# A decode-attention kernel: V trails K by two units instead of three, and older heads' projections move ahead of the last weighted sums

## The chip, the cores and the metric

The kernel runs on one core of one Trainium2 chip. The metric is the device time of one execution in microseconds, the median over several executions. The profile gives a second number, the span from the first to the last instruction.

Names used below: PE is the TensorE matmul engine, DVE is VectorE, ACT is ScalarE, POOL is GpSimd, and SP is SyncE, which issues the loads here. All times inside an execution are counted from the start of its span.

## The reference, cut to what matters

There are two independent attention blocks, A and B. Each has 2 batch entries, 32 heads, head size 192, model width 640, one new token and a cache of 8192 positions, in bf16. For each block:

```python
q = (x @ wq)                                   # [2, 1, 32*192], per head
scores = einsum("bhqd,bhkd->bhqk", q, k_cache) * 192 ** -0.5
p = softmax(scores)
o = einsum("bhqk,bhkd->bhqd", p, v_cache)      # the weighted sum
out = o.reshape(2, 1, 32*192) @ wo             # the projection
```

A pair of (head, batch entry) is a *unit*; there are 128. A unit has 3.1 MB of K and 3.1 MB of V, and each byte is used once.

## The kernel before: the parts that matter

SP issues all loads in one fixed order. Two K buffers and two V buffers hold one unit each. A load waits until its buffer is free: K until DVE has multiplied the old K by q, V until PE has finished the old weighted sum. This is the order ("LAG" is the trail of V behind K):

```python
LAG = cfg.get("LAG", 3)
LATE = LAG - 1
...
for u in range(NU):
    korder.append(("k", u))
    lag = min(1 + u // 8, LAG)        # 1, then 2, then 3
    while u - lag >= nv:
        korder.append(("v", nv)); nv += 1
for u in range(nv, NU):
    korder.append(("v", u))           # what is left: the last V, one after another
```

The work of every engine is sorted by *slot*, then by an order number within the slot. The weighted sum of unit `u` stands in PE's slot `u + LATE`. The traces show PE's work in this order, and where one instruction waited, those behind it waited too (e7 below: a projection waited 1.19 us for ACT, and PE stood idle for as long).

```python
put(pe_tab, u + LATE, 0, pe_pv(u, ...), ...)           # weighted sum: 32 matmuls
...
# near the end V is loaded in pieces, each with its own semaphore (T = 64 rows per partition)
for i, cuts in enumerate(((32, 64), (32, 64), (16, 32, 48, 64), (16, 32, 48, 56, 64))):
    PCS[NU - 4 + i] = (n0, cuts)                       # units 124, 125, 126, 127
def v_tile(u):                                         # V of the last two units goes to K buffers
    return kb[u % NK] if NU >= 8 and u >= NU - 2 else vb[u % NV]
```

Every two heads (four units) a finished group goes through five steps: ACT copies the sums out of PSUM (`f1`), PE transposes them with matmuls of one column (`f3`, 6 in the code and 12 in the trace, where each fp32 matmul shows as two passes), ACT scales by 1/sum (`f4`), and PE multiplies by `wo` (`f5`, 6 matmuls). DVE's `f2` is the reciprocal. Near the end these stand as follows. Group 30 ("older heads") covers units 120 to 123, and group 31 ("last pair") covers 124 to 127:

```python
at = u1 + 2 + LATE                                     # u1: last unit of the group
if pp == LASTP:                                        # group 31, split in three
    put(pe_tab, at - 1, 1, pe_f3h(0), ...)             # first head: after the last sum
    put(pe_tab, at - 1, 2, pe_f3h(1, (0,)), ...)       # second head, batch 0: after the last sum
    put(pe_tab, at, 1, pe_f3h(1, (1,)), ...)           # second head, batch 1
    put(act_tab, at - 1, 4, act_f4(pp, (0,)), ...)
    put(act_tab, at + 2, 3, act_f4(pp, (1,)), ...)
else:
    put(pe_tab, at, 1, pe_f3, ...)                     # group 30: between the sums of 125 and 126
    put(act_tab, at + 2, 3, act_f4(pp), ...)
put(pe_tab, at + 1, 2, pe_f5(pp), ...)                 # group 30: between the sums of 126 and 127
```

The streams of PE, DVE and ACT are emitted with hardware loops over the regular middle part. In these loops an engine waits on a semaphore against a value in a register.

Of the kernel before, what the change touches and what calls it, by code (L numbers as in the profile page):

```python
# [102 lines left out]
def build_kernel(nc, blocks, out, cfg=None):  # L103
    cfg = dict(cfg or {})
# [9 lines left out]
    NU = G * B  # L114
    scale = float(Dh) ** -0.5

    NA_MAIN = min(cfg.get("NA", 16), T - 2)
    LAG = cfg.get("LAG", 3)
    LATE = LAG - 1
    NPB = 4  # L120
    NK = cfg.get("NK", 2)
# [26 lines left out]
    with ExitStack() as es:  # L148
# [41 lines left out]
        S_pool = _Stream("pool", sem("s_pool"), reg)  # L190
        ksem = [sem(f"ksem{i}") for i in range(NK)]
        vsem = [sem(f"vsem{i}") for i in range(NV)]
        NTAIL = 13
        vtail = [sem(f"vtail{i}") for i in range(NTAIL)]
        k0sem = sem("k0sem")
        wq0sem = sem("wq0sem")
# [5 lines left out]
        def key(name, *idx):  # L202
            for i in idx:
                if i < 0:
                    return None
            return (name,) + tuple(idx)
# [6 lines left out]
            reg[("wo", w)] = (wosem, 16 * (w + 1))  # L213
        PCS = {}
        if NU >= 8:
            for i, cuts in enumerate(((32, 64), (32, 64), (16, 32, 48, 64), (16, 32, 48, 56, 64))):
                n0 = sum(len(c) for _, c in PCS.values()) if PCS else 0
                PCS[NU - 4 + i] = (n0, cuts)

        def pieces(u):  # L220
            if u not in PCS:
# [54 lines left out]
            return dma(kb[u % NK][:, ks:T, :], src[:, ks:T, :], KSPLIT[u])  # L276

        def v_tile(u):
            return kb[u % NK] if NU >= 8 and u >= NU - 2 else vb[u % NV]

        def sp_v(u, t0=0, t1=None, sm=None):
            blk, h, b, g = unit(u)
# [54 lines left out]
        def act_f1(g):  # L337
            hs = g % 2

            def fn(eng):  # L340
                eng.activation(o_sb[0:1, :, hs, :], ops[hs][0:1, :, 0:Dh], ACTF.Identity)  # L341
                return eng.activation(o_sb[32:33, :, hs, :], ops[hs][32:33, :, Dh:2 * Dh], ACTF.Identity)  # L342
            return fn

        def act_f1b(g, b):
            hs = g % 2

            def fn(eng):
                eng.activation(o_sb[0:1, b, hs, :], ops[hs][0:1, b, 0:Dh], ACTF.Identity)
                return eng.activation(o_sb[32:33, b, hs, :], ops[hs][32:33, b, Dh:2 * Dh], ACTF.Identity)  # L350
            return fn
# [47 lines left out]
        def pe_pv(u, j0, j1):  # L399
            b = u % B  # L400
            vv = v_tile(u)[:].rearrange("p (j a) d -> p j (a d)", a=2)

            def fn(eng):
                for j in range(j0, j1):
                    ins = eng.matmul(ops[(u // B) % 2][0:33, b, 0:QW], pb[u % NPB][:, j, :], vv[:, j, :],  # L405
                                     start=(j == 0), stop=(j == T // 2 - 1))
                return ins
            fn.same = (j0, j1)
            return fn
# [49 lines left out]
        def put(tab, slot, order, fn, waits, sig):  # L459
            tab[slot].append((order, len(tab[slot]), fn, waits, sig))  # L460

        for u in range(NU):
            g = u // B
            put(dve_tab, u + 1, 0, dve_d3(u), [("acc", u), ("r", u), key("ar", u - 2)], ("d3", u))
            put(dve_tab, u, 2, dve_d1a(u), [("k", u), ("a0", qg_of(u)), key("acc", u - 2)], ("d1a", u))
            put(dve_tab, u, 3, dve_d1b(u), [("k", u), ("kb", u) if u in KSPLIT else None, ("a0", qg_of(u)),
                                            key("r", u - 1)], ("d1b", u))
            put(dve_tab, u, 4, dve_lvl(u, 96), [("d1b", u)], ("l1", u))
            put(dve_tab, u, 5, dve_lvl(u, 48), [("l1", u)], ("l2", u))
            put(dve_tab, u, 6, dve_lvl(u, 24), [("l2", u)], ("l3", u))  # L470
            put(dve_tab, u, 7, dve_r(u), [("l3", u), key("d3", u - 2), key("exp", u - 2)], ("r", u))
            put(pool_tab, u + 1, 0, pool_ar(u), [("d3", u), key("nb", u - 2)], ("ar", u))
            put(pool_tab, u + 1, 1, pool_ls(u), [("exp", u), key("f2", g - 2)], ("ls", u))
            put(act_tab, u + 1, 0, act_nb(u), [("ar", u), key("exp", u - 2)], ("nb", u))
            put(act_tab, u + 1, 1, act_exp(u), [("nb", u), ("acc", u), ("r", u), key("pv", u - NPB)], ("exp", u))
            for t in range(na_of(u)):
                w = [("d1a", u), key("d3", u - 2), key("exp", u - 2)] if t == 0 else []
                put(act_tab, u, 10 + t, act_acc(u, t), w, ("acc", u) if t == na_of(u) - 1 else None)
            pc = pieces(u)
            w0 = [("exp", u), key("f1", g - 2), ("init",)]  # L480
            if pc is None:
                put(pe_tab, u + LATE, 0, pe_pv(u, 0, T // 2), w0 + [("v", u)], ("pv", u))
            else:
                for i, (t0, t1, sm) in enumerate(pc):
                    put(pe_tab, u + LATE, 0, pe_pv(u, t0 // 2, t1 // 2), (w0 if i == 0 else []) + [("vp", u, i)],
                        ("pv", u) if i == len(pc) - 1 else None)

        LASTP = G // 2 - 1 if G >= 4 else -99
        for g in range(G):
            u1 = 2 * g + 1  # L490
            pp = g // 2
            at = u1 + 2 + LATE
            w1 = [key("f3", pp - 1), ("init",)]
            if pp == LASTP and g % 2 == 0:
                put(act_tab, at + 1, 2, act_f1(g), [("pv", u1)] + w1, ("f1", g))
            elif pp == LASTP:
                put(act_tab, at - 1, 3, act_f1b(g, 0), [("pv", u1 - 1)] + w1, ("f1a", g))
                put(act_tab, at, 2, act_f1b(g, 1), [("pv", u1), ("f1a", g)], ("f1", g))
            else:
                put(act_tab, at, 2, act_f1(g), [("pv", u1)] + w1, ("f1", g))  # L500
            put(dve_tab, u1 + 2, 8, dve_f2(g), [("ls", u1), key("f4", pp - 2)], ("f2", g))
        for pp in range(G // 2):
            g1 = 2 * pp + 1
            u1 = 2 * g1 + 1
            at = u1 + 2 + LATE
            w4 = [("f2", g1 - 1), ("f2", g1), ("init",), ("wo", (2 * pp) // HG)]
            if pp == LASTP:
                put(pe_tab, at - 1, 1, pe_f3h(0), [("f1", g1 - 1), key("f4", pp - 1), ("init",)], ("f3a", pp))
                put(pe_tab, at - 1, 2, pe_f3h(1, (0,)), [("f1a", g1)], ("f3b", pp))
                put(pe_tab, at, 1, pe_f3h(1, (1,)), [("f1", g1), ("f3b", pp)], ("f3", pp))  # L510
                put(act_tab, at - 1, 4, act_f4(pp, (0,)), [("f3b", pp)] + w4, ("f4a", pp))
                put(act_tab, at + 2, 3, act_f4(pp, (1,)), [("f3", pp), ("f4a", pp)] + w4, ("f4", pp))
            else:
                put(pe_tab, at, 1, pe_f3, [("f1", g1 - 1), ("f1", g1), key("f4", pp - 1), ("init",)], ("f3", pp))
                put(act_tab, at + 2, 3, act_f4(pp), [("f3", pp), key("f5", pp - 1)] + w4, ("f4", pp))
            w = [("f4", pp), key("f5", pp - 1)]
            put(pe_tab, at + 1, 2, pe_f5(pp), w, ("f5", pp))
            if g1 % Hn == Hn - 1:
                blk = g1 // Hn
                to = at + 3 if blk == NBLK - 1 else NU - 4  # L520
                put(act_tab, to, 95, act_out(blk), [("f5", pp)], ("oev", blk))
                put(act_tab, to, 96, act_out_dma(blk, 0), [("oev", blk)], None)
                put(act_tab, to, 97, act_out_dma(blk, 1), [("oev", blk)], None)
# [7 lines left out]

        def add_v(u):
            pc = pieces(u)
            w = [("d1b", u)] if NU >= 8 and u >= NU - 2 else [key("pv", u - NV)]
            if pc is None:
                S_sp.add(sp_v(u), waits=w)
            else:
                for (t0, t1, sm) in pc:
                    S_sp.add(sp_v(u, t0, t1, sm), waits=w)
# [15 lines left out]
        for kind, u in korder:  # L555
            if kind == "k":
                if u in KSPLIT:
                    S_sp.add(sp_k(u, 0), waits=[key("d1b", u - NK)])
                    S_sp.add(sp_k(u, 1))
                else:  # L560
                    S_sp.add(sp_k(u), waits=[key("d1b", u - NK)])
                if u == 0:
                    if WQSPLIT:
                        S_sp.add(sp_wq(0, 1))
                    for blk in range(1, NBLK):
                        for b in range(B):
                            S_sp.add(sp_x(blk, b))
                w = u // UG
                if u % UG == (5 if UG >= 8 else 1):
                    S_sp.add(sp_wo(w), waits=[key("f5", (w - 1) * HG // 2)])  # L570
                if u % UG == (3 if UG >= 8 else 0) and w + 1 < NWG:
                    S_sp.add(sp_wq(w + 1), waits=[key("pq", w * HG)])
            else:
                add_v(u)
# [90 lines left out]
```

## Time and profile before

| | before |
|---|---|
| time, median of 3 executions | 1961.84 us (1961.54 to 1963.42) |
| the execution that was profiled | time 1963.61, span 1961.8 |
| bytes moved | 837 MB |
| DMA rate in the middle | 428 to 435 GB/s |
| busy: DVE, PE, ACT | 84%, 57%, 46% of the span |
| last piece of V(127) complete | 1951.70 |
| last weighted sum ends | 1955.19 |

The page of the kernel before: its first line, and the rows of 40 time slices for the DMA (tenths of busy share, then GB/s).

```profile
span 1961.8 us, 18371 instructions
...
DMA  9999999999999999999999999999999999999997
GB/s 371 429 430 431 432 430 433 431 430 433 431 433 433 429 432 433 431 433 431 432 430 431 432 430 433 431 432 428 435 432 431 432 430 433 431 432 431 432 432 299
```

The DMA's busy share is 9 tenths or more in 39 of the 40 slices, and its rate is flat: 428 to 435 GB/s in 38 of them. Only two slices are low: the first (371), where the loads start up (246 GB/s in the first 10 us), and the last (299). PE waited 774 us in all for landings of V, and DVE 236 us for landings of K. So the DMA is what the body waits for, and the end is worth looking at. This is the chain of waits of the kernel before from 1937 us on (start, duration, what; xN is the number of instructions):

```profile
1937.03 2.78 PE ops L405 x16
1939.81 2.18 PE oTps L414 x12
1941.99 6.98 PE ops L405 x32
1948.97 0.91 PE outps L441 x6
1949.88 5.31 PE ops L405 x32
1955.19 1.36 PE oTps L425 x18
...
1957.42 0.70 PE oTps L425 x6
...
1958.46 0.99 PE outps L441 x6
```

`ops L405` are weighted sums, first the second half of unit 125, then 126, then 127. `oTps L414` and `outps L441` between them are the older heads' transposes and projection. PE works without a pause although the data is there: PE, not the DMA, ends last. Two numbers describe the end:

- from the last landing to the end of the last sum: 1955.19 - 1951.70 = 3.5 us;
- from there to the end of the span: 1961.8 - 1955.19 = 6.6 us.

The landing times come from the trace's semaphore records. Each of these last loads left 16 of them, and the kernel waits for a count of 16. They are read here as one for each of the 16 DMA engines that the page counts. For the last piece the first engine was done at 1946.80, the fifteenth at 1949.39 and the sixteenth at 1951.70. The sixteenth is what the work waits for. So a load counts as landed at its sixteenth record.

### The profile page before, as it was taken

What the parts mean: (1) busy time and instruction counts of PE and PEld (TensorE: products, weight loads), DVE (VectorE), ACT (ScalarE), POOL (GpSimd) and SP (SyncE); (2) the same over time, 40 slices, a digit from 0 to 9 for tenths busy, and PEclk for the clock granted to TensorE, in tenths of its full rate; (3) what the DMA queues carried; (4) which work ended last, traced back from release to release, by engine and by line L of the source; (5) the groups of instructions that cost most, each with busy time, mean ns of one, the idle gap of its engine ahead of it and who ended that gap; (6) DMA issues with size and microseconds to landing.
All of it is one profiled execution on the core that took longest, in us unless ns stands there. A gap on an engine that the chain in (4) does not pass through costs nothing.

```text
span 1961.8 us, 18371 instructions
## 1 busy us (share of the span) xinstructions
PE 1115.6 (57%) x5004; PEld 590.1 (30%) x5004; DVE 1656.0 (84%) x962; ACT 903.0 (46%) x4743; POOL 172.8 (9%) x270
## 2 busy tenths in 40 slices
PE   2445546655566555655655556556564665556657
PEld 1222223332333223322333333223332332223324
DVE  7889898888888888898888988888888888888884
ACT  4445444445444444454444444444445444544442
POOL 3013030000001000000000000000000000000000
PEclk9777777777777777777777777777777777777778
DMA  9999999999999999999999999999999999999997
GB/s 371 429 430 431 432 430 433 431 430 433 431 433 433 429 432 433 431 433 431 432 430 431 432 430 433 431 432 428 435 432 431 432 430 433 431 432 431 432 432 299
DMA packets 56476, 837.12 MB, mean 427 GB/s; under 512 B 7416, under 2 KB 18304, under 8 KB 23680
## 3 DMA queue, kind: packets, MB, share of 16 engines
q1 hardware_dynamic: 56432, 836.79, 99.7%
q8 instruction: 12, 0.20, 0.0%
q14 instruction: 16, 0.13, 0.0%
q10 hardware_dynamic: 16, 0.01, 0.0%
HBM read 836.77 MB, written 0.01 MB: 427 GB/s over the span
## 4 chain that ended last, share of the span: by engine, by line
DMA 72%; PE 22%; DVE 5%; issue 1%; SPq 0%; ACT 0%; DVEq 0%
DMA vb<-in_B_v_cache_dram 35%; DMA vb<-in_A_v_cache_dram 29%; PE ops L405 22%; DMA kb<-in_A_k_cache_dram 8%; DVE prodD L309 3%; DVE prodD L316 1%; DVE prodA L305 0%; DVE sc L320 0%; PE oTps L414 0%; PE oTps L425 0%; PE outps L441 0%; SPq L242 0%; SPq L249 0%; DVE mp L312 0%; ACT oTzL L359 0%
## 5 line engine op out<-in xcount | busy, mean ns | idle before, releaser
L405 PE MATMUL ops<-vb,pb 128*33 128x384 bf16 x4032 | 939.9, 408 | 774.1 <-DMA vb<-in_B_v_cache_dram 387.5
L405 PEld LDWEIGHTS ops<-vb,pb 128*33 128x33 bf16 x4032 | 473.4, 120 | 1231.5 <-DMA vb<-in_B_v_cache_dram 405.8
L327 ACT ACTIVATE prodA<-prodA 128x192 bf16<-128x192 bf16 x2048 | 709.0, 350 | 117.0 <-DVE prodA L305 116.8
L309 DVE TENSOR_TENSOR prodD<-kb,qbc 128x9216 bf16<-128x9216 bf16 x128 | 633.7, 4951 | 3.6 <-DMA kb<-in_A_k_cache_dram 3.6
L316 DVE TENSOR_TENSOR prodD<-prodD 128x4608 bf16<-128x4608 bf16 (+2 forms) x384 | 599.0, 1560 | 13.3
L305 DVE TENSOR_TENSOR prodA<-kb,qbc 128x3072 bf16<-128x3072 bf16 x128 | 225.2, 1759 | 238.9 <-DMA kb<-in_B_k_cache_dram 126.9
L327 ACT ACTIVATION_READ_ACCUMULATOR prodA<-prodA 128x1 f32 x2048 | 386.9, 189 | 0.0
L331 ACT ACTIVATE nb<-mg 128x1 f32<-128x1 f32 x128 | 25.9, 203 | 737.0 <-POOL mg L292 737.0
L292 POOL PARTITION_ALL_REDUCE mg<-mp x128 | 56.3, 440 | 1637.5 <-DVE mp L312 1637.5
L320 DVE TENSOR_REDUCE sc<-prodD 128x48 f32<-128x1152 bf16 x128 | 173.2, 1353 | 4.4
L296 POOL PARTITION_ALL_REDUCE lall<-rs x128 | 105.6, 825 | 114.7 <-ACT pb L334 114.7
L387 PE MATMUL qps<-wqs,xbc 128*128 (+1 forms) x320 | 67.9, 347 | 53.4 <-ACT qbc L365 42.4
L414 PEld LDWEIGHTS oTps<-ones,o_sb 33*128 33x128 f32 x372 | 67.1, 258 | 9.8 <-issue 9.8
L414 PE MATMUL oTps<-ones,o_sb 33*128 33x1 f32 x372 | 69.8, 311 | 0.0
L341 ACT ACTIVATE o_sb<-ops 1x384 f32<-1x384 f32 x63 | 29.9, 475 | 86.0 <-PE oTps L414 75.5
L365 ACT ACTIVATE qbc<-qps 128x384 bf16<-128x384 f32 x64 | 31.3, 488 | 77.4 <-PE qps L387 76.7
L334 ACT ACTIVATE pb<-sc,nb 128x64 bf16<-128x64 f32 x128 | 52.2, 408 | 16.6 <-ACT nb L331 8.3
L387 PEld LDWEIGHTS qps<-wqs,xbc 128*128 128x128 bf16 x320 | 27.2, 101 | 88.7 <-ACT qbc L365 44.3
L312 DVE TENSOR_REDUCE mp<-sc 128x1 f32<-128x64 f32 x128 | 28.2, 220 | 13.7 <-issue 4.7
L441 PE MATMUL outps<-wos,oTz 128*4 (+1 forms) x186 | 31.1, 304 | 15.1 <-ACT oTz L359 15.1
L342 ACT ACTIVATE o_sb<-ops 1x384 f32<-1x384 f32 x63 | 30.3, 481 | 0.7
L334 ACT ACTIVATION_READ_ACCUMULATOR pb<-sc,nb 128x1 f32 x128 | 23.8, 186 | 0.0
(27 smaller groups left out, 78.1 us busy)
## 6 DMA issues: line engine op xcount, KB each, us to landing
vb<-in_A_v_cache_dram SPq DMA_DIRECT2D x64, 3072.0 KB, 22.2
kb<-in_B_k_cache_dram SPq DMA_DIRECT2D x64, 3072.0 KB, 23.0
kb<-in_A_k_cache_dram SPq DMA_DIRECT2D x63, 3072.0 KB, 22.5
vb<-in_B_v_cache_dram SPq DMA_DIRECT2D x60, 3072.0 KB, 22.8
wos<-in_A_wo_dram SPq DMA_DIRECT2D x8, 960.0 KB, 26.8
wqs<-in_B_wq_dram SPq DMA_DIRECT2D x8, 960.0 KB, 24.5
wos<-in_B_wo_dram SPq DMA_DIRECT2D x8, 960.0 KB, 26.8
wqs<-in_A_wq_dram SPq DMA_DIRECT2D x7, 960.0 KB, 24.5
```

The costliest lines, as they stand in the source:

```text
L292: return lambda eng: eng.partition_all_reduce(mg[u % 2][:], mp[u % 2][:], 128, bass.bass_isa.ReduceOp.max)
L296: return lambda eng: eng.partition_all_reduce(lall[g % 2][:, b:b + 1], rs[u % 2][:], 128, bass.bass_isa.ReduceOp.add)
L305: return lambda eng: eng.tensor_tensor(prodA[u % 2][:, 0:na, :], kb[u % NK][:, 0:na, :], qb_bc(u, na), ALU.mult)
L309: return lambda eng: eng.tensor_tensor(prodD[:, 0:T - na, :], kb[u % NK][:, na:T, :], qb_bc(u, T - na), ALU.mult)
L316: return lambda eng: eng.tensor_tensor(prodD[:, 0:nd, 0:w], prodD[:, 0:nd, 0:w], prodD[:, 0:nd, w:2 * w], ALU.add)
L320: return lambda eng: eng.tensor_reduce(sc[u % 2][:, na:T], prodD[:, 0:T - na, 0:24], AXL.X, ALU.add)
L327: return lambda eng: eng.activation(prodA[u % 2][:, t, :], prodA[u % 2][:, t, :], ACTF.Identity, accum_out=sc[u % 2][:, t:t + 1])
L334: return lambda eng: eng.activation(pb[u % NPB][:, :, ::32], sc[u % 2][:].rearrange("p (j a) -> p j a", a=2), ACTF.Exp, bias=nb[u % 2][:], ...
L365: return lambda eng: eng.activation(qbc[qg % 4][:], qps[:, 0:QW].rearrange("p (a d) -> p a d", a=2), ACTF.Identity)
L387: ins = eng.matmul(qps[:, 0:QW], xbc[blk][b][:, c, :], wqs[:, slot, c, off].rearrange("p a n -> p (a n)") if slot is not w % 2 else wqs[:, ...
L405: ins = eng.matmul(ops[(u // B) % 2][0:33, b, 0:QW], pb[u % NPB][:, j, :], vv[:, j, :], start=(j == 0), stop=(j == T // 2 - 1))
L414: ins = eng.matmul(oTps[:, 2 * i + b:2 * i + b + 1], o_sb[:, b, :, :].rearrange("p s (r i) -> p i (s r)", i=3)[:, i, :], ones33[:], start= ...
```

## The change

The intent is to have PE follow the arriving V pieces closely at the end and to leave as little as possible behind the last one. The core of the diff:

```diff
-    LAG = cfg.get("LAG", 3)
+    LAG = cfg.get("LAG", 2)
...
-            for i, cuts in enumerate(((32, 64), (32, 64), (16, 32, 48, 64), (16, 32, 48, 56, 64))):
-                PCS[NU - 4 + i] = (n0, cuts)
+            for i, cuts in enumerate(((16, 32, 48, 64), (16, 32, 48, 64), (16, 32, 48, 56, 64))):
+                PCS[NU - 3 + i] = (sum(len(c) for _, c in PCS.values()), cuts)
...      # V(126) goes to a K buffer, V(127) to the V buffer of unit 124
...      # last pair: copies, transposes and first scaling
-                put(act_tab, at + 1, 2, act_f1(g), ...)
+                put(act_tab, u1 + 3, -1, act_f1(g), ...)
-                put(act_tab, at - 1, 3, act_f1b(g, 0), ...)
+                put(act_tab, u1 + 1, 3, act_f1b(g, 0), ...)
-                put(pe_tab, at - 1, 1, pe_f3h(0), ...)
-                put(pe_tab, at - 1, 2, pe_f3h(1, (0,)), ...)
+                put(pe_tab, u1 + LATE, -1, pe_f3h(0), ...)        # before the sum of 127
+                put(pe_tab, u1 + LATE, 0.25, pe_f3h(1, (0,)), ...) # between pieces of 127
-                put(act_tab, at - 1, 4, act_f4(pp, (0,)), ...)
+                put(act_tab, u1 + 1, 4, act_f4(pp, (0,)), ...)
...      # older heads (near = group 30)
-                put(pe_tab, at, 1, pe_f3, ...)
-                put(act_tab, at + 2, 3, act_f4(pp), ...)
-            put(pe_tab, at + 1, 2, pe_f5(pp), ...)
+                put(pe_tab, at - 1 if near else at, -1 if near else 1, pe_f3, ...)    # before the sum of 124
+                put(act_tab, at if near else at + 2, 3, act_f4(pp), ...)
+                put(pe_tab, at if near else at + 1, -1 if near else 2, pe_f5(pp), ...) # before the sum of 125
...
-                if u % UG == (5 if UG >= 8 else 1):     # when the output weights are loaded
+                if u % UG == (4 if UG >= 8 else 1):
```

With a trail of two the last loads are K(127), V(125), V(126), V(127). With three they were K(127), V(124), V(125), V(126), V(127).

More of the change, by code (lines that the diff above doesn't have):

```diff
@@ L192, in build_kernel @@
         vsem = [sem(f"vsem{i}") for i in range(NV)]
-        NTAIL = 13
+        NTAIL = 15
         vtail = [sem(f"vtail{i}") for i in range(NTAIL)]
@@ L215, in build_kernel @@
         if NU >= 8:
-            for i, cuts in enumerate(((32, 64), (32, 64), (16, 32, 48, 64), (16, 32, 48, 56, 64))):
-                n0 = sum(len(c) for _, c in PCS.values()) if PCS else 0
-                PCS[NU - 4 + i] = (n0, cuts)
+            for i, cuts in enumerate(((16, 32, 48, 64), (16, 32, 48, 64), (16, 32, 48, 56, 64))):
+                PCS[NU - 3 + i] = (sum(len(c) for _, c in PCS.values()), cuts)
         def pieces(u):
@@ L278, in v_tile @@
         def v_tile(u):
-            return kb[u % NK] if NU >= 8 and u >= NU - 2 else vb[u % NV]
+            if NU >= 8 and u == NU - 2:
+                return kb[u % NK]
+            if NU >= 8 and u == NU - 1:
+                return vb[(u - 3) % NV]
+            return vb[u % NV]
         def sp_v(u, t0=0, t1=None, sm=None):
@@ L484, in build_kernel @@
                 for i, (t0, t1, sm) in enumerate(pc):
-                    put(pe_tab, u + LATE, 0, pe_pv(u, t0 // 2, t1 // 2), (w0 if i == 0 else []) + [("vp", u, i)],
+                    put(pe_tab, u + LATE, 0.1 * i, pe_pv(u, t0 // 2, t1 // 2), (w0 if i == 0 else []) + [("vp", u, i)],
                         ("pv", u) if i == len(pc) - 1 else None)
@@ L494, in build_kernel @@
             if pp == LASTP and g % 2 == 0:
-                put(act_tab, at + 1, 2, act_f1(g), [("pv", u1)] + w1, ("f1", g))
+                put(act_tab, u1 + 3, -1, act_f1(g), [("pv", u1)] + w1, ("f1", g))
             elif pp == LASTP:
-                put(act_tab, at - 1, 3, act_f1b(g, 0), [("pv", u1 - 1)] + w1, ("f1a", g))
+                put(act_tab, u1 + 1, 3, act_f1b(g, 0), [("pv", u1 - 1)] + w1, ("f1a", g))
                 put(act_tab, at, 2, act_f1b(g, 1), [("pv", u1), ("f1a", g)], ("f1", g))
@@ L506, in build_kernel @@
             w4 = [("f2", g1 - 1), ("f2", g1), ("init",), ("wo", (2 * pp) // HG)]
+            w5 = [("f4", pp), key("f5", pp - 1)]
             if pp == LASTP:
-                put(pe_tab, at - 1, 1, pe_f3h(0), [("f1", g1 - 1), key("f4", pp - 1), ("init",)], ("f3a", pp))
-                put(pe_tab, at - 1, 2, pe_f3h(1, (0,)), [("f1a", g1)], ("f3b", pp))
+                put(pe_tab, u1 + LATE, -1, pe_f3h(0), [("f1", g1 - 1), key("f4", pp - 1), ("init",)], ("f3a", pp))
+                put(pe_tab, u1 + LATE, 0.25, pe_f3h(1, (0,)), [("f1a", g1)], ("f3b", pp))
                 put(pe_tab, at, 1, pe_f3h(1, (1,)), [("f1", g1), ("f3b", pp)], ("f3", pp))
-                put(act_tab, at - 1, 4, act_f4(pp, (0,)), [("f3b", pp)] + w4, ("f4a", pp))
+                put(act_tab, u1 + 1, 4, act_f4(pp, (0,)), [("f3b", pp)] + w4, ("f4a", pp))
                 put(act_tab, at + 2, 3, act_f4(pp, (1,)), [("f3", pp), ("f4a", pp)] + w4, ("f4", pp))
+                put(pe_tab, at + 1, 2, pe_f5(pp), w5, ("f5", pp))
             else:
-                put(pe_tab, at, 1, pe_f3, [("f1", g1 - 1), ("f1", g1), key("f4", pp - 1), ("init",)], ("f3", pp))
-                put(act_tab, at + 2, 3, act_f4(pp), [("f3", pp), key("f5", pp - 1)] + w4, ("f4", pp))
-            w = [("f4", pp), key("f5", pp - 1)]
-            put(pe_tab, at + 1, 2, pe_f5(pp), w, ("f5", pp))
+                near = pp == LASTP - 1
+                put(pe_tab, at - 1 if near else at, -1 if near else 1, pe_f3,
+                    [("f1", g1 - 1), ("f1", g1), key("f4", pp - 1), ("init",)], ("f3", pp))
+                put(act_tab, at if near else at + 2, 3, act_f4(pp), [("f3", pp), key("f5", pp - 1)] + w4, ("f4", pp))
+                put(pe_tab, at if near else at + 1, -1 if near else 2, pe_f5(pp), w5, ("f5", pp))
             if g1 % Hn == Hn - 1:
@@ L533, in add_v @@
             pc = pieces(u)
-            w = [("d1b", u)] if NU >= 8 and u >= NU - 2 else [key("pv", u - NV)]
+            w = [key("pv", u - NV)]
+            if NU >= 8 and u == NU - 2:
+                w = [("d1b", u)]
+            if NU >= 8 and u == NU - 1:
+                w = [("pv", u - 3)]
             if pc is None:
```

## The prediction

> **What bounds the kernel now.** The DMA. The page shows a mean DMA share of 9 tenths or more in 39 of 40 slices and 430 to 433 GB/s in nearly all of them; 837 MB have to be moved. [...] DVE is busy 84% and PE 57%, and both wait for landings. So reordering can shorten only head and tail.
>
> **The body (units 16 to about 123).** A unit moves 6.3 MB in about 14.6 us. Today V(u-3) follows K(u) and the sum of u stands in slot u+2; afterwards V(u-2) follows K(u) and the sum stands in slot u+1. Seen from the transfers, PE does the same work at the same time, and buffers come free as before. The scores of u are ready about 14.3 us after K(u) lands (timeline), V(u) lands about 36 us after K(u). No new wait. Gain 0.
>
> **The head.** The trace shows PE waiting 15.5, 17.0 and 13.6 us for ACT in the first 155 us. The new slots remove most of this, but the windows show DMA share 1.0 from 10 us on, so it is worth about 0.
>
> **The tail.** In the timeline PE works without a break from 1937.03 to 1956.54, with data waiting: sum of unit 125's second half 2.78, older heads' transpose 2.18, unit 126's sum 6.98, older heads' output projection 0.91, unit 127's sum 5.31 (ends at 1955.19), transposes 1.36. The landings in the trace: the last piece of V(127) is complete at 1951.70 (its first engine was done at 1946.80; one engine trails). [...] So 3.5 us of PE work lie behind the last byte, then 6.6 us to the end (1961.8).
>
> After: three V instead of four follow the last K; older heads' transpose (2.18) and projection (0.91) are done before the last sums; two of three parts of the last transpose (estimate 0.9 and 0.45) go ahead of, or between, the last pieces. K(127) lands about 7.3 us later, at about 1929; its softmax is then done at about 1944, before the first piece of V(127) (1946.1). PE then follows the pieces: a piece of 8 matmuls costs 1.3 us at full clock and about 1.9 throttled, pieces come every 1.83 us. The last sum should end about 1.3 us after the last landing (at about 1953), and the chain behind it shrinks from 6.6 to about 5.0 us (copy 0.6, transpose 0.75, scale 0.3, projection 1.0, output copy 0.45, output DMA 1.9). Landings stay: same bytes, as many pieces.
>
> Sum: 1961.8 - 2.2 - 1.6 = **1958 us**, range 1955 to 1961. Chances: faster by over 2%: 0.005; within 2%: 0.99; slower: 0.005.
>
> **What would show it.** Right: last V landing within 1 us of 1951.7 and body slices unchanged; PE's last sum waits for the DMA piece by piece; the chain of waits goes from the last V piece through few matmuls into copy, transpose, projection. Wrong: PE's last sum waits for the last softmax (K(127) late), or PE is still running without a break behind the pieces at a throttled clock, or body slices lose GB/s.
>
> **What would make it wrong.** A lower PE clock in the last 10 us (32 matmuls took 5.3 to 8.2 us), a different trail of the slowest DMA engine, or the last softmax later than 1946.

The sum came to 1958.0 us: from 1961.8 it takes 2.2 us (3.5 to 1.3, behind the last landing) and 1.6 us (6.6 to 5.0, the chain after it).

## The result, and the profile after

The time is 1958.24 us, the median of 4 executions (1957.15 to 1959.41), against 1961.69 (1960.63 to 1963.42, 4 executions) before. The ratio is 0.9982, with a 95% interval of 0.9964 to 0.9999, just clear of 1. The difference of the medians is 3.45 us; the prediction's was 3.8.

The page of the kernel after, its first line and the GB/s of the slices:

```profile
span 1955.3 us, 18519 instructions
...
GB/s 385 430 433 428 433 431 432 433 430 432 431 432 432 431 434 430 432 433 429 432 430 433 431 430 433 431 431 434 429 433 430 432 433 432 431 429 435 432 433 338
```

The middle is unchanged. The first slice is 14 GB/s higher and the last 39. The chain of waits of the kernel after, its end:

```profile
1928.14 18.52 DMA vb<-in_B_v_cache_dram
...
1946.71 1.48 PE ops L408 x8
1948.19 0.61 PE oTps L428 x6
1948.80 1.42 PE ops L408 x8
...
1950.95 0.70 PE oTps L428 x6
...
1951.99 0.99 PE outps L444 x6
```

Now a DMA landing at 1946.67 (the third of V(127)'s five pieces) is on the chain, and behind it stand only 16 matmuls of the last sum and three transposes (6 passes). The last piece landed at 1948.53 and the last sum ended at 1950.22, 1.7 us behind it. From there to the end are 5.1 us.

| profiled executions | before | after | difference |
|---|---|---|---|
| last landing | 1951.70 | 1948.53 | -3.2 |
| last landing to end of the last sum | 3.5 | 1.7 | -1.8 |
| end of the last sum to end of the span | 6.6 | 5.1 | -1.5 |
| span | 1961.8 | 1955.3 | -6.5 |

The profiled pair differs by 6.5 us and the medians by 3.45. So about half of what the pair shows, the earlier last landing, needs an explanation of its own. Adding up the packets of the load queue in the order of their ends shows where most of that half comes from: 15 MB had been moved 1.7 us earlier in the kernel after (40.86 against 42.60), and 1.6 to 2.0 us separate the two at 50, 500 and 834 MB. At 4 MB (14.08 us) there was no gap yet, at 10 MB it was 1.5 us (29.18 against 30.73). The windows view of that stretch, for the kernel before (PE, PE's weight loads, DVE, ACT and POOL busy with their counts; the last three numbers are the clock granted to PE as a share of full speed, the DMA share and GB/s):

```profile
15.00:30.00 15.00, 1.78 (x5) 0.59 (x5) 14.76 (x8) 3.24 (x20) 9.18 (x4) 1.00 0.99 378
```

and for the kernel after:

```profile
15.00:30.00 15.00, 0.00 (x0) 0.00 (x0) 14.76 (x8) 3.06 (x19) 9.13 (x4) 0.50 0.99 423
```

The DMA is busy in both, at 378 and 423 GB/s. The loads issued up to 33 us are the same ones in the same order, at times that differ by 0.04 us or less. Either the change causes this in some other way, or it is chance. The experiments below show which.

### The profile page after: what moved, and what is told of

The parts are those of the page before. It is cut to its first block, busy times and chain, and to the rows that moved or that the text cites. A ratio compares the mean times of both kernels' runs of the same rounds, so it can differ in the third digit from the quotient of the medians.

```text
span 1955.3 us, 18519 instructions
## 1 busy us (share of the span) xinstructions
PE 1110.9 (57%) x5004; PEld 588.5 (30%) x5004; DVE 1656.2 (85%) x962; ACT 903.2 (46%) x4743; POOL 165.8 (8%) x270
## 4 chain that ended last, share of the span: by engine, by line
DMA 74%; PE 23%; DVE 2%; issue 0%; SPq 0%; ACT 0%; DVEq 0%
DMA vb<-in_B_v_cache_dram 37%; DMA vb<-in_A_v_cache_dram 33%; PE ops L408 23%; DMA kb<-in_A_k_cache_dram 4%; DVE prodD L312 2%; DVE prodD L319 1%; DVE prodA L308 0%; DVE sc L323 0%; SPq L241 0%; PE oTps L428 0%; PE outps L444 0%; SPq L248 0%; DVE mp L315 0%; ACT out_sb L372 0%; ACT o_sb L353 0%
## 5 line engine op out<-in xcount | busy, mean ns | idle before, releaser
L299 POOL PARTITION_ALL_REDUCE lall<-rs x128 | 101.3, 791 | 111.1 <-ACT pb L337 111.1
## 6 DMA issues: line engine op xcount, KB each, us to landing
kb<-in_B_k_cache_dram SPq DMA_DIRECT2D x64, 3072.0 KB, 22.4
kb<-in_A_k_cache_dram SPq DMA_DIRECT2D x63, 3072.0 KB, 22.4
```

Source lines behind the costliest of these rows:

```text
L299: return lambda eng: eng.partition_all_reduce(lall[g % 2][:, b:b + 1], rs[u % 2][:], 128, bass.bass_isa.ReduceOp.add)
```

## The experiments

Every experiment has its loops written out, before and after included:

```diff
-                S_dve.emit(eng, 8)      # likewise ACT with 8, PE with 4
+                S_dve.emit(eng)
```

This keeps every instruction and its order, but it costs about 16 us (see the first run). The written-out kernels are therefore compared with each other, mainly by the two numbers defined above, which do not depend on when the last V landed. They do depend on PE's clock, so they are taken up again behind the table of all ends. Four runs share a chip: e1 to e4, e5 to e8 and e9 to e12. All outputs were correct.

**Theory A**, from the prediction: what gains is the work taken away from between and behind the last sums. **Rival B**: the shorter trail gains, since three V instead of four come in a row. **Rival C**: the shorter trail removes PE's stalls in the head and so gains 1.8 us of DMA time there.

### e1: the kernel before, written out

> The kernel before with its loops written out (so that every semaphore wait is on a constant), the control. My theory: same work, same order, so 1961 us give or take 3 [...]; from the last V landing to the end about 10 us at a throttled PE clock, 8.5 at full clock (in the looped kernel 1961.8 - 1951.70 = 10.1). Rival (written-out code is a different kernel): over 10 us away.

It measured 1978.4 us (1976.77 to 1978.68), 0.75% over the looped kernel in its rounds. On the time the rival held: it is 16 us more, not within 3, so the written-out kernel is another one as far as its time goes. From the last landing (1966.70) to the end of the span (1976.7) it is 10.0 us, as in the looped kernel (10.1), so the end can be studied in this form. The 16 us come with a later last landing, 1966.70 instead of 1951.70; more about it at the end.

### e2: the shorter trail alone

```diff
-    LAG = cfg.get("LAG", 3)
+    LAG = cfg.get("LAG", 2)
```

> Before, written out, with only the trail of V behind K set to 2 units (all tail placements, V buffers and pieces as before). Theory A (the gain is the moved projections): same as the written-out before within 1 us; the older heads' 12 transposes still stand between the sums of units 125 and 126 and their 6 projections between those of 126 and 127; last landing to end 8 to 10 us. Rival B (the shorter trail is what gains, three V instead of four at the end): 3 us faster, last landing to end near 7 us. Rival C (the shorter trail takes PE stalls out of the head, which gains 1.8 us of DMA time): the DMA has moved 50 MB 1.6 us earlier than in the written-out before.

It measured 1978.3 us (1977.81 to 1979.06), equal to e1. From the last landing (1965.84) to the end (1976.0) it is 10.2 us. PE stood idle for 7.6 us until the first half of V(125) had landed behind K(127), and the sum of unit 125 then took 8.20 us, where one at full clock takes 5.31. The loads had moved 50 MB at 122.53 us, against 121.91 in e1. The shorter trail alone gains nothing, neither at the end (against B) nor in the head (against C).

### e3: the new end with the old trail

This is the kernel after, written out, with these two lines put back:

```diff
-    LAG = cfg.get("LAG", 2)
+    LAG = cfg.get("LAG", 3)
...
-                if u % UG == (4 if UG >= 8 else 1):
+                if u % UG == (5 if UG >= 8 else 1):
```

> After, written out, with V three units behind K as before (and the output weights loaded at the old place), but all the tail placements, buffers and pieces of after. Theory A: as fast as the written-out after within 1 us, about 3.4 us under the written-out before; last landing to end about 6.8 us. Rival B (the shorter trail gains): near the written-out before, last landing to end 9 us or more.

It measured 1977.92 us (1976.94 to 1979.16), 0.5 us under e1. From the last landing (1967.46) to the end (1976.1) it is 8.6 us. Theory A missed: it said 6.8. The chain of waits of e3:

```profile
1924.08 20.96 DMA vb<-in_B_v_cache_dram
...
1945.09 7.29 PE ops L408 x32
1952.38 0.91 PE outps L444 x6
1953.29 10.51 PE ops L408 x64
```

PE worked without a break from 1945.09 to 1970.97. It began only when V(124) had landed whole at 1945.04, 22.4 us before the last landing, since the new cuts leave V(124) in one piece. With the old trail V(124) stands right in front of the last three V, and PE then has 25.9 us of work for 22.4 us of arrivals. Of these 25.9 us, 2.0 are half clock: the 32 matmuls of unit 124, which followed 3.6 us of idle PE, took 7.29 us and not 5.31, and the clock record shows 0.50 until 1949.02. The chain behind the last sum is the new one, 5.1 us, but the last sum ends 3.5 us late, as before. That led to **theory D**: with pieces of 8 matmuls PE needs 1.48 us for what arrives in 1.84 us, so it has some 0.35 us to spare in each piece. What matters is that it starts each sum early enough to use that. An estimate from the same numbers leaves a second reading open: without the 2.0 us of half clock the last sum would have ended 1.6 us behind the last landing, as in e4 below.

### e4: the kernel after, written out

> The kernel after, written out. Theory A: 3.4 us (2.5 to 4.5) under the written-out before, last landing to end 6.8 us as in the looped one (1955.3 - 1948.53). Rival C (the head gains with the change): DMA has moved 50 MB 1.6 us earlier than in the written-out before; theory A says the difference there is chance and has either sign, under 1 us on average.

It measured 1975.15 us (1974.54 to 1975.65), 3.25 us under e1 on the same chip, and the two sets of five executions do not overlap. From the last landing (1966.66) to the end (1973.4) it is 6.7 us. 50 MB of loads were moved at 122.51 us, against 121.91 in e1. So the gain of 3.3 us is all in the end, and the head gains nothing with the change. Theory A held here, C did not.

### e5: the new cuts and buffers, all projections at their old places

This is e4 with the copies, transposes and scalings of the last pair back behind the last sum, and the older heads not moved:

```diff
-                put(act_tab, u1 + 3, -1, act_f1(g), ...)
+                put(act_tab, at + 1, 2, act_f1(g), ...)
-                put(act_tab, u1 + 1, 3, act_f1b(g, 0), ...)
+                put(act_tab, at - 1, 3, act_f1b(g, 0), ...)
-                put(pe_tab, u1 + LATE, -1, pe_f3h(0), ...)
-                put(pe_tab, u1 + LATE, 0.25, pe_f3h(1, (0,)), ...)
+                put(pe_tab, at - 1, 1, pe_f3h(0), ...)
+                put(pe_tab, at - 1, 2, pe_f3h(1, (0,)), ...)
-                put(act_tab, u1 + 1, 4, act_f4(pp, (0,)), ...)
+                put(act_tab, at - 1, 4, act_f4(pp, (0,)), ...)
...
-                near = pp == LASTP - 1
+                near = False
```

> Written out, trail of two units, the new pieces and V buffers of after, but every projection and transpose at the place where before has it (older heads' 12 transposes behind the sum of unit 125, their 6 projections behind that of 126, the last pair's transposes all at the end). Theory D, formed after the first four runs (PE has 0.35 us to spare in each piece of 1.84 us, so it catches up with moved or unmoved extra work if the sums are cut finely; with 3.1 us of extra work it is just caught up at the end): last landing to end about 7.6 us. Theory A (the moved projections are what gains): 9.5 to 10 us, as in the run with the trail alone (10.2).

It measured 1976.93 us (1975.97 to 1977.73). From the last landing (1966.35) to the end (1975.2) it is 8.9 us, which lies between D (7.6) and A (9.5 to 10). The last sum ended 2.1 us behind the last landing, instead of 3.6 in e2. The chain of waits of e5 shows why it was not less:

```profile
1951.58 1.48 PE ops L408 x8
1953.05 2.18 PE oTps L417 x12
1955.23 6.99 PE ops L408 x32
1962.22 0.91 PE outps L444 x6
1963.13 5.31 PE ops L408 x32
```

The 32 matmuls of unit 126 took 6.99 us and those of 127 took 5.31. The windows view gives the granted clock as 0.57 from 1955 to 1959 and 1.00 from 1959 on, so a step of half clock cost 1.7 us. Without it PE would have had to wait for the third piece of V(127), which landed at 1964.44; with the 2.8 us that PE takes from there (e6 shows them) the last sum would have ended 0.9 us behind the last landing, and the end would have been 7.5 to 7.7 us, which is D's number. That is an estimate. The new cuts and buffers, which were not tested apart, shorten the first number from 3.6 us to 2.1 as measured, which the prediction did not count. As e2 and e5 both hold half clock, the size is open: without it the estimates are 1.7 and 0.9.

### e6: e5 plus the older heads moved ahead

This is e5 with `near = pp == LASTP - 1`.

> As after, written out, but only the older heads' transposes and projections are ahead; the last pair's transposes are all behind the last sum as in before. Last sum ends about 1.0 us behind the last landing (pieces of 4 matmuls, PE waits for each), then the chain of 6.6 us: last landing to end 7.6 us by theory A and D alike, 0.9 us more than after. If only the older heads' move matters: 6.8.

It measured 1977.01 us (1975.89 to 1978.45), so in time it equals e5. In the profile the last sum ended 0.9 us behind the last landing (1969.23 - 1968.32), as expected. The chain behind it took 7.5 us instead of 6.6, however: the last six projection matmuls took 1.77 us and not 0.99, at half clock. From the last landing to the end it is 8.4 us. The chain of waits of e6, the last 16 matmuls of the sum and the last projection:

```profile
1966.46 2.78 PE ops L408 x16
...
1972.52 1.77 PE outps L444 x6
```

Moving the older heads alone frees PE but did not shorten the run by anything that can be measured, and the 0.9 us is what e5 is estimated at without its half clock.

This run also answers the question about the head. Its program starts like that of e5, on the same chip. The windows view of e6:

```profile
15.00:30.00 15.00, 0.00 (x0) 0.00 (x0) 14.76 (x8) 3.58 (x21) 9.43 (x4) 1.00 0.98 375
```

375 GB/s, and 421 in e5. Of the 14 profiles two had this slow start (before with 378, e6 with 375), and the other twelve had 419 to 428, among them the written-out kernel before (421). So it comes and goes without the change, for a reason that no run shows. The first pair of profiles happened to have it on one side, and there it was worth 1.6 to 2.0 us.

### e7: e4 with the older heads back at their old places

```diff
-                near = pp == LASTP - 1
+                near = False
```

> As after, written out, but the older heads' transposes and projections stand where before has them, between the last sums; the last pair's transposes are split and ahead as in after. Theory D: the 3.1 us of older work plus 1.75 us of early transposes outrun the spare time of the pieces, the last sum ends 2.4 us behind the last landing, chain 5.1: last landing to end 7.5 us, 0.8 us more than after. Theory A: 3.1 us more than after, 9.8 us.

It measured 1978.5 us (1976.69 to 1979.82), no better than e1. From the last landing (1966.26) to the end (1977.0) it is 10.7 us. Both theories missed, because the mixture has a wait that neither kernel has. Its chain of waits:

```profile
1961.22 0.32 ACT o_sb L353
...
1961.57 0.43 ACT oTz L362 x2
...
1962.04 0.98 PE outps L444 x6
```

On ACT the last pair's early copy (`o_sb`), which needs the sum of unit 126, now stands ahead of the older heads' scaling (`oTz`), which the older heads' projection on PE waits for. PE idles 1.2 us for that, and 24 matmuls of unit 127 then took 5.7 us at a reduced clock. The run does not say what the last pair's move is worth alone. It does show that the two moves belong together: the last pair can go ahead only if the older heads have gone before it on ACT as well.

### e8: the new end with the old trail, V(124) in two pieces

This is e3 with

```diff
-            for i, cuts in enumerate(((16, 32, 48, 64), (16, 32, 48, 64), (16, 32, 48, 56, 64))):
-                PCS[NU - 3 + i] = ...
+            for i, cuts in enumerate(((32, 64), (16, 32, 48, 64), (16, 32, 48, 64), (16, 32, 48, 56, 64))):
+                PCS[NU - 4 + i] = ...
```

> As the run with the new tail at a trail of three units, and V of unit 124 loaded in two pieces as before has it. That run missed (last landing to end 8.6 us, not 6.8): PE worked 25.9 us without a break from the landing of the whole V 124, which came 22.4 us before the last. Theory D: with V 124 in halves PE starts 3.7 us earlier and is caught up by the end: last landing to end 6.8 us as in after, time within 1 us of the written-out after. Rival B (the K between V 124 and V 125 is needed to catch up, so the shorter trail is part of the gain): 8 us or more.

It measured 1975.64 us (1975.04 to 1976.57); e4, on another chip, had 1975.15. From the last landing (1967.19) to the end (1974.0) it is 6.8 us. Its chain of waits:

```profile
1949.69 15.63 DMA vb<-in_B_v_cache_dram
...
1965.37 1.48 PE ops L408 x8
1966.85 0.61 PE oTps L428 x6
1967.46 1.42 PE ops L408 x8
```

The end is that of the kernel after, step by step. Theory D held and rival B fell: a trail of three does as well, if V(124) is cut so that PE can begin it early. Unit 124 met half clock here too (7.00 us), but PE had begun it 3.3 us earlier than in e3 and was waiting for pieces again from unit 126 on. What the shorter trail provides is a K load between V(124) and V(125), in which PE finishes V(124), so that V(124) need not be cut.

### e9 and e10: does the older heads' transpose lower PE's clock?

In the clock records of the kernels before and after, PE's clock is either 1.00 or 0.50, and each record but the last lasts 3.41 us or a whole multiple of it (248 and 252 records); such a 3.41 us is called a step here. Half clock came where PE was idle: in the kernel before no matmul ran from 110 to 120 us, and the granted clock there was 0.50. But it also came where PE was not idle. Two lines of the windows view of the kernel before:

```profile
1940.00:1943.00 3.00, 3.00 (x19) 2.60 (x19) 0.00 (x0) 0.96 (x4) 0.00 (x0) 1.00 1.02 426
1943.00:1946.00 3.00, 3.00 (x12) 1.44 (x11) 0.00 (x0) 0.29 (x1) 0.00 (x0) 0.54 1.00 416
```

PE is busy all the time and the granted clock falls to 0.54, the mean from 1943 to 1946 us. In before, e1, e5 and e8 this followed the older heads' 12 transposes of one column (2.2 us). In e2 and e7, which have them between the last sums as well, it did not (so it is four of six kernels, not four of five as the expectation below has it). Theory H was that such a stretch of matmuls brings on the half clock; a reason for it was not shown. Two twins of e4 with extra work behind the sum of unit 125 were to test it:

```diff
+        # e9: 12 fp32 transposes of one column       e10: 26 matmuls of 384 columns
+            ins = eng.matmul(qps[:, 0:1], dz[:], ones33[:], start=True, stop=True)
+            ins = eng.matmul(qps[0:33, 0:QW], pb[u % NPB][:, j, :], vv[:, j, :], start=True, stop=True)
```

> After, written out, plus 12 more transposes of one column (each two passes in fp32, about 4.36 us of PE work) behind the sum of unit 125; result unused, outputs stay right. Theory H, formed from the clock of the first eight profiles (the PE clock went to half for 3.4 us after the older heads' 12 transposes in four of five kernels that have them between the last sums, and in none that has them earlier[...]): the clock is at half for one 3.4 us step right after the added block, the sum of unit 126 takes about 7.0 us instead of 5.3, last landing to end about 10.4 us. Rival (chance, or work without a break lowers the clock): no half clock here more than in the dense twin; 8.7 us.

> The twin of the run with added transposes: 26 more matmuls of 384 columns (about 4.3 us) at the same place, into an unused bank; outputs stay right. Theory H: the clock stays at full through all of the last sums, the sum of unit 126 takes 5.3 us, last landing to end about 8.7 us. Rival (work without a break lowers the clock): half clock here as well, about 10.4 us.

e9 measured 1976.31 us (1975.25 to 1977.66) and e10 measured 1976.54 (1976.22 to 1976.94). In both, the clock was 1.00 through all the last sums, and unit 126 took 5.3 and 5.2 us. From the last landing to the end it is 7.1 us in e9 (1974.0 - 1966.92) and 8.4 in e10 (1974.4 - 1965.99). e10 came out near its 8.7, and in it, as in e3 and e9, no half clock followed work without a break. Theory H predicted a half clock in e9 and none came. The added block was also shorter than planned (2.77 us for 24 passes). By the clock records it lay 1.8 us in one step and 0.9 in the next, whereas in before, e1, e5 and e8 at least 2.1 us of transposes fell into one step, and half clock followed in the next. In e2 and e7, where none followed, a step boundary divided the transposes as well (1.0 and 1.2 us, 0.8 and 1.3). This fits H, but it was seen only afterwards. So e9 neither confirms nor clears the transposes. What puts the clock to half in this stretch stays open. It decides about 1.7 us of the end of a single execution.

### e11: a trail of one unit

```diff
-    LAG = cfg.get("LAG", 2)
+    LAG = cfg.get("LAG", 1)
```

> After, written out, with a trail of one unit. The prediction says that the last softmax comes 14.3 us behind the landing of the last K; with two units that is before the last V's first piece. With one unit the last K lands 14.7 us before the last V piece, the softmax ends 0.4 us before it, so the last sum waits for the softmax: it starts about at the last landing minus 0.4, ends 5.6 us behind it; last landing to end 10.7 us, about 4 us slower than the written-out after. Rival (the softmax has slack even then): 6.8 us. In the body no change (430 GB/s).

It measured 1983.51 us (1982.44 to 1985.69), 8.4 us more than e4 (another chip). From the last landing (1966.95) to the end (1981.6) it is 14.7 us. The direction was right, the size was not (10.7 us and about 4 us slower had been expected). A part of its chain of waits:

```profile
1954.48 1.67 DVE prodA L308
...
1968.20 0.45 ACT pb L337 x2
...
1968.70 5.76 PE ops L408 x24
```

The last softmax ends at 1968.65, 14.2 us after the first product with K(127) starts, as the prediction had it, and PE waits for it. Two things add to that. DVE starts that product at 1954.5 although K(127) landed at 1952.04, since it was still behind with unit 126. The 24 matmuls that follow took 5.8 us instead of 4.0. Together these are 4.2 us, about the 3.9 us that were missing. So at a trail of two the last softmax has room, and at one it has not.

### e12: the early transposes moved further ahead

```diff
-                put(pe_tab, u1 + LATE, -1, pe_f3h(0), ...)
-                put(pe_tab, u1 + LATE, 0.25, pe_f3h(1, (0,)), ...)
+                put(pe_tab, u1 + LATE - 1, 0.15, pe_f3h(0), ...)    # between pieces of 126
+                put(pe_tab, u1 + LATE, 0.05, pe_f3h(1, (0,)), ...)  # after the first piece of 127
```

> After, written out, with the two early transposes of the last pair moved further ahead: the first heads' 6 between the second and third piece of the sum of 126, the second's 3 behind the first piece of the sum of 127. PE then has spare time for them; the last sum ends 1.0 us behind the last landing instead of 1.65, chain 5.05 as before: last landing to end 6.1 us instead of 6.7. In the time 0.6 us of 1975, under the spread of the runs.

It measured 1974.46 us (1974.09 to 1974.63); e4, on another chip, had 1975.15. From the last landing (1966.80) to the end (1972.8) it is 6.0 us, as expected. Its chain of waits:

```profile
1964.93 2.79 PE ops L408 x16
```

Nothing but matmuls of the sum stands behind the third piece. By the profile this is 0.7 us better than the kernel after.

### All ends side by side

| kernel | last landing | last sum ends behind it | from there to the end | both | time |
|---|---|---|---|---|---|
| before (looped) | 1951.70 | 3.5 | 6.6 | 10.1 | 1961.69 |
| after (looped) | 1948.53 | 1.7 | 5.1 | 6.8 | 1958.24 |
| e1 before, written out | 1966.70 | 3.4 | 6.6 | 10.0 | 1978.4 |
| e2 trail of two alone | 1965.84 | 3.6 | 6.6 | 10.2 | 1978.3 |
| e3 new end, trail of three | 1967.46 | 3.5 | 5.1 | 8.6 | 1977.92 |
| e4 after, written out | 1966.66 | 1.6 | 5.1 | 6.7 | 1975.15 |
| e5 new cuts alone (trail of two) | 1966.35 | 2.1 | 6.8 | 8.9 | 1976.93 |
| e6 e5 + older heads ahead | 1968.32 | 0.9 | 7.5 | 8.4 | 1977.01 |
| e7 e5 + last pair ahead | 1966.26 | 5.6 | 5.1 | 10.7 | 1978.5 |
| e8 e3 + V(124) in halves | 1967.19 | 1.7 | 5.1 | 6.8 | 1975.64 |
| e12 halves earlier | 1966.80 | 0.9 | 5.1 | 6.0 | 1974.46 |

The first four columns are of one profiled execution each. e1 to e4 ran on one chip, e5 to e8 on a second, e12 on a third.

Half clock moves the second column. 32 matmuls of a sum take 5.31 us at full clock (unit 127 of before, at a granted clock of 1.00). Unit 126 took 6.98 us in before and 6.99 in e1 and e5, unit 125 took 8.20 in e2 and unit 124 took 7.29 in e3, and in none of them did PE wait for a piece after that. (The 5.6 us of e7 hold half clock as well, in unit 127.) Without this excess the last sum would have ended about 1.8 us behind the last landing in before, 1.7 in e1 and e2, 1.6 in e3 and 0.9 in e5. These are estimates from the times of the matmuls and of the landings. In after, e4 and e8, unit 124 met half clock too (8.2, 7.9 and 7.0 us), but PE had caught up before the last sum. So the new end leaves room for a slow stretch, and the old one did not have it. How much of the gain in this column is the order of the work itself and how much is half clock that no longer counts, the profiles do not separate. The third column, 6.6 or 5.1 us, does not have this doubt except in e5 and e6, whose last projection met half clock.

## Why the prediction was right, point by point

- **The time.** 1958.0 predicted, 1958.24 measured, a saving of 3.8 predicted and 3.45 measured. The agreement to 0.3 us is partly luck. The prediction subtracted from 1961.8, which is the *span* of a profiled execution whose time was 1963.61. That execution was 1.9 us slower than the median, and time exceeds span by 1.8 us. The two errors cancelled. Moreover, the 3.5 us that it started from hold 1.7 us of half clock of that one execution (unit 126, 6.98 us), which it counted as PE's work like the rest.
- **The DMA bounds the body, which can't gain.** Right: 428 to 435 GB/s in the middle slices after, as before, and the gap of 1.6 to 2.0 us between the two profiles, once opened in the head, stays through the body.
- **The head is worth 0.** Right. PE's waits for ACT in the first 200 us, up to 17.0 us before, are down to 0.6 us and less, and the DMA did not gain. The 1.6 to 2.0 us that the first pair of profiles shows there are a slow start that two of 14 profiles have, e6 with the new trail among them.
- **The end.** Right in sum: 3.5 to 1.3 and 6.6 to 5.0 were predicted, 3.5 to 1.7 and 6.6 to 5.1 measured. The last sum ends later than predicted because three transposes (0.61 us) stand behind the third piece of V(127) on the chain; e12 took them away and measured 0.9.
- **What makes the end shorter.** Here the prediction's split was off. It put the 2.2 us down to the older heads' 2.18 and 0.91 us of work and took the pieces as the same ("same bytes, as many pieces"). e5 has the new cuts and buffers with the shorter trail and all projections at their old places, and its first number is 2.1 us where e2 has 3.6. With the older heads moved as well (e6) it is 0.9, but e5 without its half clock is estimated at 0.9 too, and the two took the same time. So moving the older heads alone is not shown to gain anything; it is what lets the last pair go ahead (e7). The early transposes of the last pair give the 1.5 us in the chain, and they cost the sum 0.7 us (1.6 in e4, 0.9 in e6). In time, on the same chip, both moves together are worth 1.3 us (e8 against e5, 1975.64 against 1976.93; e8 also has the old trail). The prediction also counted "three V instead of four follow the last K" among the reasons: e2 and e8 show that this alone is worth nothing.
- **The last softmax is done before the last V's first piece.** Right: it ended at 1940.6, the piece landed at 1942.94. e11 shows what happens when it is not.
- **PE waits piece by piece.** Right for units 125 and 126: the timeline of the kernel after has waits of 0.3 to 0.46 us ahead of their pieces. In the last sum itself, of which the prediction spoke, PE waited only once, 0.24 us for the third piece, because the early transposes had used up the spare time.
- **Last landing within 1 us of 1951.7.** Wrong: 1948.53. Of the 3.2 us, 1.6 to 2.0 are the slow start of the profiled execution of before. Most of the rest is the sixteenth DMA engine, which trailed the fifteenth by 2.3 us there and by 0.9 us in the profile of after.

## What to carry to other kernels

Here the DMA moved 428 to 435 GB/s through the body of the kernel, before and after, and reordering won only what lay behind the last byte (10.1 us to 6.8). So measure that piece directly: last landing to the end of the last dependent work, and from there to the end. Cut the last loads finely enough that the consumer starts early and keeps a little spare time per piece (0.35 us of 1.84 here), then put other work into that spare time or ahead of it, and check on every engine what the moved work now stands behind (in e7 that was 1.2 us of idle PE). Read the clock records of both profiles, too: here one step of half clock (1.7 us) is as large as the gain in the first number (1.8 us). When two profiles differ by more than the medians do, look for chance in a part that the change does not touch before explaining it.

## What the runs leave open

- Writing out the loops, with the same instructions in the same order, made the kernel 0.75% slower (1978.4 against 1962.7 us). The pages show 39 and 51 packets of instructions instead of 12 and 16 (1.06 MB instead of 0.33), and the last landing moved from 1951.7 to 1966.7. In the last V piece of e4, the fifteenth DMA engine was done at 1957.69 and the sixteenth at 1966.66. No run shows whether the added packets delay this engine or the loads, so the cause of the 16 us stays open.
- The clock fell to half from 1943.3 to 1946.7 us in the kernel before with PE busy from 1937.03 on, and 32 matmuls took 6.98 us instead of 5.31. No run shows what brings the half clock on; whether matmuls of one column do, e9 did not settle.
- In the last piece of V the sixteenth DMA engine trailed the fifteenth by 0.9 to 2.3 us in the looped kernels and by 1.1 to 9.8 us in the written-out ones, and this delay enters the time directly here, where the work on the last piece ends the program. Why it trails, no run shows.
- The slow start has no cause yet: in two of 14 profiles, with the same loads, the DMA moved 375 and 378 GB/s between 15 and 30 us, instead of 419 to 428, at a busy share of 0.98 and more.
